# Cosine attention and a highway layer: transposing transfers joined, small work spread over three engines, order rewritten

## The chip, the core and the metric

The kernel runs on one core of one Trainium2 chip. A core has TensorE (PE, matmuls), VectorE (DVE), ScalarE (ACT), GpSimd (POOL) and SyncE (SP, used here to issue DMAs). Each engine works through its own queue in order and waits at semaphores for the others. The metric is the device time of one execution in microseconds; the median of three executions is given.

## The reference

```python
def _attn_ref(q, k, v, tau):                 # q, k, v: (8, 12, 448, 64), float32
    q_n = q / (np.linalg.norm(q, axis=-1, keepdims=True) + 1e-06)
    k_n = k / (np.linalg.norm(k, axis=-1, keepdims=True) + 1e-06)
    scores = np.matmul(q_n, k_n.transpose(0, 1, 3, 2)) / tau
    attn = np.exp(scores - np.max(scores, axis=-1, keepdims=True))
    attn = attn / (np.sum(attn, axis=-1, keepdims=True) + 1e-09)
    return np.matmul(attn, v)

def _moe_ref(x, w_h, w_t, b_t):              # x: (3584, 768), from the attention
    H = np.maximum(x @ w_h, 0.0)
    T = 1.0 / (1.0 + np.exp(-(x @ w_t + b_t)))
    return T * H + (1.0 - T) * x
```

Attention over 8 batches of 12 heads, with q and k brought to length one, and then a gated layer of 768 by 768 on its output.

## The kernel before

**Tiling.** The twelve heads of a batch are worked in six pairs, 48 pairs in all (pair s = 6b + p). The 448 rows of a head are 384 main rows, three to a partition, and a tail of 64. `load_main` brings q and k of a batch in one DMA each from GpSimd's queue (tiles qr, kr, cast to fp16; three buffers each), `load_tails` brings the tails from SP's queue (qt, kt), `load_v` both parts of v (vr, vt).

**Preparation of a batch.** `square` squares q and k for three pairs at a time (tile sq, three buffers; L374 on VectorE, L373 on ScalarE in batch 0), `tail_squares` the tails on ScalarE (L399); `folds` adds the squares up (f at L388 and L390, the last sum at L392); `steps` makes the reciprocal square root, by logarithm and exponential on ScalarE in batch 0, by Newton steps on VectorE after that (rs). `scaled` multiplies q and k of a pair by it on GpSimd (tile qn, L499, four buffers, one pair each), `qtnorm` the tails of q (qtn, L509, GpSimd), `ktnorm` those of k (kb, L518, VectorE). `vcast` and `vtcast` copy v into the tile vp with a column of ones (L626 and L632: VectorE for the main rows of batch 0, ScalarE for the rest).

**Transposes.** In batches 0 to 3 `turn` transposes a pair on TensorE (L540, L543) and copies it out on VectorE (qT, L547). In batches 4 to 7 (`BY_DMA`) it is a transposing DMA on SP's queue: six blocks of 128 by 128 for each pair (L532), and for each batch three blocks of q tails (qtT, L555) and six of k tails (kbT, L558).

**Attention of a pair.** `scores`: three groups of score matmuls (L600) and one for the tail (L614), each followed by its exponential on ScalarE (E at L606, Et at L618). `attend`: the product with v and the row sums (L644, L648, L664), a reciprocal and the division on VectorE (L672, L674) into x, one tile for each batch, in four buffers.

**The layer.** `ffn` takes a batch's x in three groups of 128 rows of 768 and one of the tails. x is transposed (tile xT, three buffers, one group each): by DMA on SP's queue in batches 1 to 6, six or three blocks at a time (L704), by TensorE and VectorE in batches 0 and 7. Matmuls with both weights (L745, tails L729), a tanh on ScalarE for the gate (L768, L769), the relu less x on VectorE (L782), the gate and its product (L787, L790), the sum with x on GpSimd (out, L795; VectorE at the very end), the store from SP's queue (L805, tails in two stores at L801).

**Order.** All of this is first listed as operations (`Plan.op`), each with an engine and what it reads and writes. `ORDER` then gives the order in which all 1723 are issued, and `SLOTS` the buffer that each new tile takes. So the order on every engine and queue is written out by hand, operation by operation. Operations marked `port` on VectorE and GpSimd get one more rule: a GpSimd operation waits for the last marked VectorE operation ahead of it in the order, and where it is in the set `URGENT` the next marked VectorE operation waits for it.

Of the kernel before, what the change touches and what calls it, by code (L numbers as in the profile page):

```python
# [9 lines left out]
FP16 = mybir.dt.float16  # L10
# [92 lines left out]
""".replace("\n", "")  # L103
)

URGENT = frozenset(
    int(n)
    for n in """
116 135 154 155 225 310 336 337 394 413 485 583 621 736 774 811 877 945 963 998 1080 1106 1140 1147 1166 1237
1268 1283 1298 1369 1387 1405 1440 1471 1553 1554 1571 1589 1590 1607 1608 1643 1691  # L110
""".split()
)


class Op:
# [801 lines left out]
```

## Time and profile before

| | |
|---|---|
| median of three executions | 275.48 us (273.61 to 279.13) |
| profiled execution | 274.65 us |
| its span, first to last instruction | 272.8 us |
| granted TensorE clock | 0.994 of full speed |
| chain of waits, by engine | PE 53%, DVE 17%, DMA 14%, ACT 5%, POOL 3%, issue 3%, SP's queue 2% |
| read from and written to memory | 37.82 and 11.01 MB |
| exponentials of the main scores (L606) | 144, 128.5 us of ACT |

The profile comes from one execution. Busy time of an engine is the time in which one of its instructions ran; in a group's row stand the count, the busy time, the mean of one in ns, and behind the second bar the engine's idle time just before them with what ended it. A PE that is busy isn't at its peak, since matmuls overlap: the same kind of matmul shows 323 ns in its row and comes every 82 ns where nothing disturbs it. The chain of waits follows the work that ended last back to what released it, step by step.

### The profile page before, as it was taken

The numbers are of one execution on the slowest core, as the hardware profiler recorded it, in microseconds if no ns is written. First come the engines' busy times: TensorE is split into PE (matmuls) and PEld (weight loads), VectorE is DVE, ScalarE is ACT, GpSimd is POOL, SyncE is SP. The second block draws the span as 40 slices with busy tenths as digits, with TensorE's granted clock in tenths as the row PEclk, the third lists the DMA queues.
The fourth block names the chain that finished last, engine by engine and source line by source line (L and its number), as shares of the span: only waits on it lengthen the run. The fifth ranks groups of instructions, "written<-read, shape, count | busy, mean of one in ns | idle before, by whom it ended". The sixth has DMA issues, their size and how long they took to land.

```text
span 272.8 us, 9106 instructions
## 1 busy us (share of the span) xinstructions
PE 243.6 (89%) x3783; PEld 163.2 (60%) x3783; DVE 198.2 (73%) x446; ACT 209.6 (77%) x312; POOL 159.1 (58%) x172
## 2 busy tenths in 40 slices
PE   0467898999999999999999897998899999999990
PEld 0235475766775676666656574665566767677650
DVE  6577989999989889976876778629853454446464
ACT  2479999879896998789689898797798995683120
POOL 5979656585584775576766564558667464300540
PEclk9999999999999999999999999999999999999997
DMA  7999999999859999996999989999795749620243
GB/s 131 221 192 191 180 207 202 186 194 198 105 78 176 209 164 119 150 171 128 210 157 151 173 191 181 143 190 222 173 167 86 116 124 191 204 90 2 60 178 113
DMA packets 104249, 43.13 MB, mean 158 GB/s; under 512 B 98064, under 2 KB 101136, under 8 KB 104208
## 3 DMA queue, kind: packets, MB, share of 16 engines
q0 software_dynamic: 38464, 16.32, 49.3%
q1 hardware_dynamic: 64512, 25.80, 48.7%
q8 instruction: 30, 0.49, 0.7%
q10 hardware_dynamic: 1232, 0.43, 0.6%
q14 instruction: 11, 0.09, 0.1%
HBM read 37.82 MB, written 11.01 MB: 179 GB/s over the span
## 4 chain that ended last, share of the span: by engine, by line
PE 53%; DVE 17%; DMA 14%; ACT 5%; POOL 3%; issue 3%; SPq 2%; POOLq 0%; ACTq 0%; DVEq 0%
PE pS L745 24%; PE pS L600 7%; PE pB L648 7%; PE pS L729 4%; DMA qT<-qn 4%; DMA qr<-in_q_dram 4%; DMA out_dram<-os 3%; PE pB L664 3%; PE pB L614 3%; PE pB L644 3%; DVE sq L374 2%; POOL qn L499 2%; DMA kr<-in_k_dram 2%; DVE f L388 2%; ACT E L606 2%
## 5 line engine op out<-in xcount | busy, mean ns | idle before, releaser
L606 ACT ACTIVATE E<-pS 128x896 f16<-128x896 f32 x144 | 128.5, 920 | 21.0 <-PE pS L600 18.0
L745 PEld LDWEIGHTS <-xT 64*128 64x128 f16 x1152 | 52.9, 94 | 33.6 <-issue 2.2
L795 POOL TENSOR_TENSOR os<-x,hm 128x768 f32<-128x768 f16 (+1 forms) x30 | 44.2, 1479 | 41.6 <-DVE hm L790 28.5
L745 PE MATMUL pS<-wt,xT 64*128 64x384 f16 x576 | 58.6, 323 | 0.6 <-DMA xT<-x 0.6
L745 PE MATMUL pS<-wh,xT 64*128 64x384 f16 x576 | 57.5, 323 | 0.0
L499 POOL TENSOR_TENSOR qn<-kr,rs 128x384 f16<-128x384 f16 x47 | 39.1, 841 | 30.4 <-DVE rd L672 10.4
L499 POOL TENSOR_TENSOR qn<-qr,rs 128x384 f16<-128x384 f16 x47 | 38.9, 832 | 22.9 <-DVE hm L790 8.3
L600 PE MATMUL pS<-qT 64*128 64x384 f16 x288 | 44.1, 327 | 3.8 <-DMA qT<-qn 1.7
L648 PE MATMUL pB<-vp,E 128*128 128x65 f16 x864 | 43.6, 194 | 0.0
L782 DVE SCALAR_TENSOR_TENSOR hm<-pS,x 128x768 f16<-128x768 f32 (+1 forms) x33 | 27.4, 833 | 19.8 <-PE pS L745 13.6
L648 PEld LDWEIGHTS <-E 128*128 128x128 f16 x864 | 38.5, 98 | 1.2 <-issue 0.7
L600 PEld LDWEIGHTS <-qT 64*128 64x128 f16 x576 | 23.2, 94 | 21.7 <-issue 7.8
L644 PE MATMUL pB<-vp,Et 128*128 128x130 f16 x144 | 32.0, 222 | 0.8 <-ACT Et L618 0.6
L769 ACT ACTIVATE tt<-pS 128x768 f16<-128x768 f32 x24 | 19.5, 813 | 16.3 <-PE pS L745 15.0
L618 ACT ACTIVATE Et<-pB 128x512 f16<-128x512 f32 x48 | 28.5, 603 | 2.9 <-PE pB L614 2.7
L674 DVE SCALAR_TENSOR_TENSOR x<-pB,rd 128x448 f16<-128x448 f32 x48 | 29.7, 620 | 1.1
L600 PE MATMUL pS<-qtT,qT 64*128 64x64 f16 x282 | 27.6, 189 | 0.0
L672 DVE RECIPROCAL rd<-pB 128x7 f32<-128x7 f32 x48 | 9.5, 200 | 22.7 <-PE pB L648 14.4
L280 PE MATMUL pB<-fill 128*128 128x384 f16 x40 | 9.6, 367 | 13.3 <-DVE fill L251 10.7
L626 ACT COPY vp<-vr 128x384 f16<-128x384 f16 x42 | 21.1, 515 | 0.0
L790 DVE TENSOR_TENSOR hm<-tt,hm 128x768 f16<-128x768 f16 (+1 forms) x32 | 18.3, 581 | 2.8 <-POOL os L795 2.6
L664 PE MATMUL pB<-vp,E 128*128 128x65 f16 x288 | 18.3, 194 | 0.2 <-DVE x L674 0.2
(95 smaller groups left out, 382.3 us busy)
## 6 DMA issues: line engine op xcount, KB each, us to landing
out_dram<-os SPq DMA_DIRECT2D x24, 384.0 KB, 3.7
vr<-in_v_dram POOLq DMA_DIRECT2D x8, 576.0 KB, 9.6
kr<-in_k_dram POOLq DMA_DIRECT2D x7, 576.0 KB, 9.8
qr<-in_q_dram POOLq DMA_DIRECT2D x7, 576.0 KB, 11.4
qt<-in_q_dram SPq DMA_DIRECT2D x16, 96.0 KB, 5.8
vt<-in_v_dram SPq DMA_DIRECT2D x16, 96.0 KB, 5.0
out_dram<-os SPq DMA_DIRECT2D x16, 96.0 KB, 2.4
kt<-in_k_dram SPq DMA_DIRECT2D x14, 96.0 KB, 4.9
```

What stands on the lines that cost most here:

```text
L499: return e.tensor_mul(R("qn", s)[:, t].rearrange("l c ab d -> l ab c d"), rows(t, b, p, p + 1)[:, :, 0, :].rearrange("l ab (c d) -> l ab c ...
L600: ins = nc.tensor.matmul(dst, lhsT=qT[ln, 384 + 128 * c : 512 + 128 * c], rhs=rhs, start=True, stop=True)
L606: return nc.scalar.activation(R("E", s)[:, c, :, 0:448], R("S", 3 * s + c)[:, :, 0:448], AF.Exp, scale=inv_tau)
L618: op("ACT", f"expt {s}", lambda: nc.scalar.activation(R("Et", s)[:, 64:576], R("B", ("S", s))[:, :], AF.Exp, scale=inv_tau), key + 3, r=[( ...
L626: return nc.vector.tensor_copy(dst, src) if b == 0 else nc.scalar.copy(dst, src)
L644: nc.tensor.matmul(U[:, 2 * c : 2 * c + 2, :].rearrange("p g e -> p (g e)"), lhsT=Et[:, 128 + 128 * c : 256 + 128 * c], rhs=vp[:, 6:8, :]. ...
L648: ins = nc.tensor.matmul(U[:, 2 * c + ab, :], lhsT=EF[:, j, 576 * ab + 128 * c : 576 * ab + 128 * c + 128], rhs=vp[:, 3 * ab + j, :], star ...
L664: ins = nc.tensor.matmul(U[:, 6, :], lhsT=lt, rhs=rh, start=(n == 0), stop=(n == 7))
L674: op("DVE", f"ev {s}", lambda: nc.vector.scalar_tensor_tensor(out=R("x", b)[:, :, D * p : D * p + D], in0=U_()[:, :, 0:D], scalar=0.0, in1 ...
L745: ins = nc.tensor.matmul(P[:, h, 0:MH], lhsT=lt, rhs=rh, start=(part == 0 and cc == (-1 if wi == 0 else 0)), stop=(part == 1 and cc == CC ...
L782: return nc.vector.scalar_tensor_tensor(out=o_, in0=i0, scalar=0.0, in1=xs, op0=ALU.max, op1=ALU.subtract)
L795: op(en, f"out{wd} {g}", lambda: eng.tensor_add(R("os", g)[:, 0:W], xall(), R("hm", g)[:, 0:W]), at + 0.1, r=[("gg", g), ("x", b)], w=[("o ...
```

## The change

**Transfers joined.** qn now holds two pairs in a tile (two buffers, still four pairs), qT two pairs (three buffers, six pairs for four), and one transposing DMA of twelve blocks turns both. The tails of q stand behind those of k in one tile kb, and one transfer of nine blocks turns them into one tile tT. xT holds two groups in a tile (two buffers), and x of a batch goes in a transfer of twelve blocks and one of nine. The tail rows of the result are stored in one DMA for two.

**Engines.** A set `MOVED` names 146 operations that go to another engine than their usual one; `pick(one, other)` looks it up as an operation is listed. The usual engine of v's copies and of the tail squares in batches 0 or 1 changes too. In numbers, before and after:

| operations | before | after |
|---|---|---|
| products of q and k (L499) | POOL 94, DVE 2 | POOL 45, DVE 51 |
| tails of q; of k (halves) | POOL 8; DVE 16 | POOL 2, DVE 6; DVE 7, POOL 9 |
| squares of three pairs, half each | DVE 28, ACT 2 | DVE 15, ACT 15 |
| squares of tails | ACT 16 | ACT 12, DVE 4 |
| sums of squares (L388, L390) | DVE 46 | DVE 34, POOL 12 |
| copies of v (main); (tails) | ACT 42, DVE 6; ACT 16 | ACT 20, DVE 24, POOL 4; ACT 8, DVE 6, POOL 2 |
| copies of a transposed pair (L547) | DVE 24 | DVE 18, ACT 6 |
| sums with x (full; tails) | POOL 23, DVE 1; POOL 7, DVE 1 | POOL 10, DVE 14; POOL 5, DVE 3 |
| clears of E, Et, kb | DVE 8 | DVE 1, POOL 7 |

**Buffers and order.** x goes from four buffers to three. The product with v waits for the clears of all three E and Et buffers, for one of each before. `ORDER`, `SLOTS` and `URGENT` (43 operations before, 57 after) are new throughout; there are 1687 operations for 1723.

```diff
-    NR = dict(qr=3, kr=3, qt=2, kt=2, kb=2, vr=3, vt=2, vp=2, sq=3, f1=2, f2=2, n2=2, rs=3, qn=4,
-              qtn=2, qtT=2, qT=4, kbT=2, E=3, Et=3, rd=2, x=4, xT=3, tt=3, hm=3, os=4, S=3, B=2)
+    NR = dict(qr=3, kr=3, qt=2, kt=2, kb=2, vr=3, vt=2, vp=2, sq=3, f1=2, f2=2, n2=2, rs=3, qn=2,
+              qT=3, tT=2, E=3, Et=3, rd=2, x=3, xT=2, tt=3, hm=3, os=4, S=3, B=2)
...
+    def pick(one, other):
+        return other if len(pl.ops) in MOVED else one
+    def product(eng, out_, a, c):
+        return (nc.vector if eng == "DVE" else nc.gpsimd).tensor_mul(out_, a, c)
+    def copied(eng, out_, a):
+        return nc.scalar.copy(out_, a) if eng == "ACT" else (nc.vector if eng == "DVE" else nc.gpsimd).tensor_copy(out_, a)
...
+            eng = pick(eng, "DVE" if eng == "ACT" else "POOL" if b == 1 else "ACT")
...
     def scaled(t, b, p, key, eng):
         s = 6 * b + p
-        e = nc.vector if eng == "DVE" else nc.gpsimd
+        eng = pick(eng, "DVE")
...
         if b in BY_DMA:
-            op("SP", f"xd6 q {s}", lambda: nc.sync.dma_start(
-                R("qT", s)[:, 0:768].rearrange("p (c l) -> p c l", c=6), R("qn", s).rearrange("l t c ab d -> l (t c ab d)"),
-                transpose=True), key, r=[("qn", s)], w=[("qT", s)])
+            if p % 2 == 0:
+                m = s // 2
+                op("SP", f"xd12 q {m}", lambda: nc.sync.dma_start(
+                    R("qT", m)[:, 1:13, :], R("qn", m).rearrange("l x t c ab d -> l (x t c ab d)"),
+                    transpose=True), key, r=[("qn", m, 0), ("qn", m, 1)], w=[("qT", m, 0), ("qT", m, 1)])
             return
...
-            op("SP", f"xd3 t {b}", lambda: nc.sync.dma_start(
-                R("qtT", b)[:, :, :], R("qtn", b).rearrange("l j ab d -> l (j ab d)"), transpose=True), key,
-               r=[("qtn", b)], w=[("qtT", b)])
-            op("SP", f"xd6 k {b}", lambda: nc.sync.dma_start(
-                R("kbT", b)[:, :, :], R("kb", b).rearrange("l p ab d -> l (p ab d)"), transpose=True), key,
-               r=[("kb", b)], w=[("kbT", b)])
+            op("SP", f"xd9 t {b}", lambda: nc.sync.dma_start(
+                R("tT", b)[:, :, :], R("kb", b).rearrange("l p ab d -> l (p ab d)"), transpose=True), key,
+               r=[("kb", b, 0), ("kb", b, 1)], w=[("tT", b)])
...
+        eng = pick(*(("DVE", "POOL") if b < 2 else ("ACT", "DVE")))
...
-            op("SP", f"xd{nb} {g}", lambda: nc.sync.dma_start(R("xT", g)[:, 0:nb, :], xall(), transpose=True), key,
-               r=[("x", b)], w=[("xT", g)])
+            if not i % 2:
+                hf = i // 2
+                nd = 12 - 3 * hf
+                op("SP", f"xd{nd} {b} {hf}", lambda: nc.sync.dma_start(
+                    R("xT", (b, hf))[:, 0:nd, :], R("x", b)[:, 4 * hf : 4 + 3 * hf, :].rearrange("l h m -> l (h m)"),
+                    transpose=True), key, r=[("x", b)], w=[("xT", (b, hf), 0), ("xT", (b, hf), 1)])
...
-            for h in range(2):
-                op("SP", f"sth {g} {h}", lambda h=h: nc.sync.dma_start(
-                    rows_[384:448, MH * h : MH * h + MH], R("os", g)[64 * h : 64 * h + 64, 0:MH]), at + 0.4,
-                   r=[("os", g)], w=[("o", g)])
+            op("SP", f"sth {g}", lambda: nc.sync.dma_start(
+                rows_[384:448].rearrange("l (h m) -> h l m", h=2), R("os", g)[:, 0:MH]), at + 0.4,
+               r=[("os", g)], w=[("o", g)])
```

More of the change, by code (lines that the diff above doesn't have):

```diff
@@ L108 @@
     for n in """
-116 135 154 155 225 310 336 337 394 413 485 583 621 736 774 811 877 945 963 998 1080 1106 1140 1147 1166 1237
-1268 1283 1298 1369 1387 1405 1440 1471 1553 1554 1571 1589 1590 1607 1608 1643 1691
+225 241 316 336 355 374 443 482 523 542 561 599 618 649 678 688 729 748 766 767 805 823 824 869 884 894 934 1003
+1004 1051 1065 1080 1090 1148 1164 1183 1199 1200 1218 1247 1261 1276 1319 1326 1344 1360 1361 1482 1515 1521
+1539 1540 1557 1574 1575 1591 1592
+""".split()
+)
+MOVED = frozenset(
+    int(n)
+    for n in """
[6 rows of a table added]
 """.split()
@@ L213 @@
         rs=ring("rs", NR["rs"], [128, 3, NN], FP32),
-        qn=ring("qn", NR["qn"], [128, 2, NCH, 2, D], FP16),
-        kbT=ring("kbT", NR["kbT"], [128, NP, 128], FP16),
-        qtn=ring("qtn", NR["qtn"], [128, 3, 2, D], FP16),
-        qtT=ring("qtT", NR["qtT"], [128, 3, 128], FP16),
-        qT=ring("qT", NR["qT"], [128, 896], FP16),
+        qn=ring("qn", NR["qn"], [128, 2, 2, NCH, 2, D], FP16),
+        tT=ring("tT", NR["tT"], [128, NP + 3, 128], FP16),
+        qT=ring("qT", NR["qT"], [128, 14, 128], FP16),
         E=ring("E", NR["E"], [128, NCH, 2, 512], FP16),
@@ L237, with squared @@
     op = pl.op
+    def pick(one, other):
[4 more added lines that the diff above has]
+        return nc.scalar.copy(out_, a) if eng == "ACT" else (nc.vector if eng == "DVE" else nc.gpsimd).tensor_copy(out_, a)
+    def squared(eng, out_, a):
+        return nc.scalar.activation(out_, a, AF.Square) if eng == "ACT" else product(eng, out_, a, a)
     def R(name, i):
@@ L248, in clear, with fn @@
         for n, t in enumerate(tiles):
-            def fn(t=t):
+            eng = pick("DVE", "POOL") if name in ("zE", "zEt", "zvp", "zkb") else "DVE"
+            e = nc.vector if eng == "DVE" else nc.gpsimd
+            def fn(t=t, e=e):
                 for vw, x in views(t):
-                    ins = nc.vector.memset(vw, x)
+                    ins = e.memset(vw, x)
                 return ins
-            op("DVE", f"{name} {n}", fn, key + gap * n, w=[(name, n)])
+            op(eng, f"{name} {n}", fn, key + gap * n, w=[(name, n)])
     op("POOL", "ident", lambda: make_identity(nc, ident), 5, w=[("id", 0)])
@@ L371, in fn @@
                 d = R("sq", i)[:, g0:g1, :].rearrange("l (p a c) d -> l a p (c d)", a=4, c=NCH)[:, 2 * t : 2 * t + 2]
-                if eng == "ACT":
-                    return nc.scalar.activation(d, a, AF.Square)
-                return nc.vector.tensor_mul(d, a, a)
+                return squared(eng, d, a)
             op(eng, f"sq{p1 - p0} {b} {p0} {t}", fn, key,
-               r=[rowtok(t, b, p) for p in range(p0, p1)] + ([("tab", 0)] if eng == "ACT" else []), w=[("sq", i)], port=eng == "DVE")
+               r=[rowtok(t, b, p) for p in range(p0, p1)] + [("tab", 0)], w=[("sq", i)], port=eng != "ACT")
         if tails:
@@ L387, in folds @@
         w0, w1 = ("fa",) + i, ("fb",) + i
-        op("DVE", f"fa{n} {b} {i[1]}", lambda: nc.vector.tensor_add(v_("f1"), v_("sq")[:, :, 0:32], v_("sq")[:, :, 32:64]),
+        eng = pick("DVE", "POOL")
+        e1 = nc.vector if eng == "DVE" else nc.gpsimd
+        op(eng, f"fa{n} {b} {i[1]}", lambda: e1.tensor_add(v_("f1"), v_("sq")[:, :, 0:32], v_("sq")[:, :, 32:64]),
            key, r=[("sq", i)], w=[w0], u=[("f1", i)], port=True)
-        op("DVE", f"fb{n} {b} {i[1]}", lambda: nc.vector.tensor_add(v_("f2"), v_("f1")[:, :, 0:16], v_("f1")[:, :, 16:32]),
+        eng = pick("DVE", "POOL")
+        e2 = nc.vector if eng == "DVE" else nc.gpsimd
+        op(eng, f"fb{n} {b} {i[1]}", lambda: e2.tensor_add(v_("f2"), v_("f1")[:, :, 0:16], v_("f1")[:, :, 16:32]),
            key, r=[w0], w=[w1], u=[("f1", i), ("f2", i)], port=True)
@@ L395, in tail_squares, with fn @@
     def tail_squares(b, i, key):
-        def fn(t):
+        def fn(t, eng):
             sq = R("sq", i)[:, 6 * t : 6 * t + 6].rearrange("l g d -> l (g d)")
             a = R("qt", b).rearrange("l ab p d -> l (ab p d)") if t == 0 else R("kt", b).rearrange("l p d -> l (p d)")
-            return nc.scalar.activation(sq, a, AF.Square)
+            return squared(eng, sq, a)
         for t in range(2):
-            op("ACT", f"sqt {b} {t}", lambda t=t: fn(t), key, r=[("qt", b) if t == 0 else ("kt", b)] + ([("tab", 0)] if b == 0 else []),
-               w=[("sq", i)])
+            eng = pick(*(("DVE", "POOL") if b == 1 else ("ACT", "DVE")))
+            op(eng, f"sqt {b} {t}", lambda t=t, eng=eng: fn(t, eng), key,
+               r=[("qt", b) if t == 0 else ("kt", b)] + ([("tab", 0)] if b == 0 else []), w=[("sq", i)], port=eng != "ACT")
     def square_tail(b, key):
@@ L495, in scaled @@
         s = 6 * b + p
-        e = nc.vector if eng == "DVE" else nc.gpsimd
+        eng = pick(eng, "DVE")
         def fn():
-            return e.tensor_mul(
-                R("qn", s)[:, t].rearrange("l c ab d -> l ab c d"),
+            return product(
+                eng, R("qn", s // 2)[:, s % 2, t].rearrange("l c ab d -> l ab c d"),
                 rows(t, b, p, p + 1)[:, :, 0, :].rearrange("l ab (c d) -> l ab c d", c=NCH),
@@ L505, in scaled, with fn @@
         op(eng, f"{'qk'[t]}n {s}", fn, key, r=[rowtok(t, b, p), ("rn", b, p)], u=[("rs", b)],
-           w=[("qn", s)], port=True)
+           w=[("qn", s // 2, s % 2)], port=True)
     def qtnorm(b, key):
-        op("POOL", f"qtn {b}", lambda: nc.gpsimd.tensor_mul(
-            R("qtn", b).rearrange("l j ab d -> l ab j d"), R("qt", b)[:, :, :, :],
+        eng = pick("POOL", "DVE")
+        op(eng, f"qtn {b}", lambda: product(
+            eng, R("kb", b)[:, NP : NP + 3].rearrange("l j ab d -> l ab j d"), R("qt", b)[:, :, :, :],
             rtails(b).unsqueeze(3).to_broadcast([128, 2, 3, D])), key, r=[("qt", b), ("rn", b, 6)],
-           u=[("rs", b)], w=[("qtn", b)], port=True)
+           u=[("rs", b)], w=[("kb", b, 1)], port=True)
     def ktnorm(b, key):
         for ab in range(2):
-            def fn(ab=ab):
+            eng = pick("DVE", "POOL")
+            def fn(ab=ab, eng=eng):
                 ln = slice(64 * ab, 64 * ab + 64)
-                return nc.vector.tensor_mul(R("kb", b)[ln, :, ab, :], R("kt", b)[ln, :, :],
+                return product(eng, R("kb", b)[ln, 0:NP, ab, :], R("kt", b)[ln, :, :],
                                             R("rs", b)[ln, 0, 6:12].unsqueeze(2).to_broadcast([64, NP, D]))
-            op("DVE", f"kb {b} {ab}", fn, key, r=[("kt", b), ("zkb", min(b, 1)), ("rn", b, 6)], u=[("rs", b)],
-               w=[("kb", b)], port=True)
+            op(eng, f"kb {b} {ab}", fn, key, r=[("kt", b), ("zkb", min(b, 1)), ("rn", b, 6)], u=[("rs", b)],
+               w=[("kb", b, 0)], port=True)
     tn = [0]
@@ L610, in ft @@
         def ft():
-            qT, S_ = R("qT", s), R("B", ("S", s))
-            keys = R("kbT", b)[:, p] if b in BY_DMA else qT[:, 768:896]
-            for dst, rhs in ((S_[:, 0:64], tails()), (S_[:, 64:448], qT[:, 0:384]), (S_[:, 448:512], tails())):
+            S_ = R("B", ("S", s))
+            qT = R("qT", s // 2)[:, 1 + 6 * z : 4 + 6 * z].rearrange("p c l -> p (c l)")
+            keys = R("tT", b)[:, p] if b in BY_DMA else R("qT", s // 2)[:, 13 * z]
+            for dst, rhs in ((S_[:, 0:64], tails()), (S_[:, 64:448], qT), (S_[:, 448:512], tails())):
                 ins = nc.tensor.matmul(dst, lhsT=keys, rhs=rhs, start=True, stop=True)
             return ins
-        op("PE", f"qkt {s}", ft, key + 3, mode="F", r=tok + ([("kbT", b)] if b in BY_DMA else []), w=[("B", ("S", s))])
+        op("PE", f"qkt {s}", ft, key + 3, mode="F", r=tok, w=[("B", ("S", s))])
         op("ACT", f"expt {s}", lambda: nc.scalar.activation(
@@ L625, in fn @@
             dst = R("vp", b)[:, p, 0:6, 0:D].rearrange("l (ab c) d -> l ab c d", ab=2)
-            return nc.vector.tensor_copy(dst, src) if b == 0 else nc.scalar.copy(dst, src)
-        op("DVE" if b == 0 else "ACT", f"vc {b} {p}", fn, key, r=[("vr", b), ("zvp", min(b, 1))], w=[("vp", b, p)], port=b == 0)
+            return copied(eng, dst, src)
+        op(eng, f"vc {b} {p}", fn, key, r=[("vr", b), ("zvp", min(b, 1))], w=[("vp", b, p)], port=eng != "ACT")
     def vtcast(b, key):
         for ab in range(2):
-            op("ACT", f"vtc {b} {ab}", lambda ab=ab: nc.scalar.copy(
-                R("vp", b)[64 * ab : 64 * ab + 64, :, 6 + ab, 0:D], R("vt", b)[64 * ab : 64 * ab + 64, :, :]),
-               key, r=[("vt", b), ("zvp", min(b, 1))], w=[("vp", b, 6)])
+            eng = pick(*(("DVE", "POOL") if b < 2 else ("ACT", "DVE")))
+            op(eng, f"vtc {b} {ab}", lambda ab=ab, eng=eng: copied(
+                eng, R("vp", b)[64 * ab : 64 * ab + 64, :, 6 + ab, 0:D], R("vt", b)[64 * ab : 64 * ab + 64, :, :]),
+               key, r=[("vt", b), ("zvp", min(b, 1))], w=[("vp", b, 6)], port=eng != "ACT")
     def attend(b, p, key):
@@ L666, in tail @@
             return ins
-        rd = [("E", s), ("Et", s), ("vp", b, p), ("vp", b, 6), ("zE", min(s, 2)), ("zEt", min(s, 2))]
+        rd = [("E", s), ("Et", s), ("vp", b, p), ("vp", b, 6)] + [(z, n) for z in ("zE", "zEt") for n in range(3)]
         for c in range(NCH):
@@ L793, in ffn @@
         last = b == B - 1 and i >= 2
-        eng, en = (nc.vector, "DVE") if last else (nc.gpsimd, "POOL")
+        en = "DVE" if last else pick("POOL", "DVE")
+        eng = nc.vector if en == "DVE" else nc.gpsimd
         op(en, f"out{wd} {g}", lambda: eng.tensor_add(R("os", g)[:, 0:W], xall(), R("hm", g)[:, 0:W]), at + 0.1,
```

71 lines of the change are left out of this document (38 added, 33 removed), and 140 rows, old and new, of tables (MOVED, ORDER).

## The prediction

> **What bounds the kernel now.** I read the page first, for the engines' totals, then the table of windows for where TensorE stands still, then the chain of waits inside those windows, then the groups for prices.
>
> ```profile
> PE 243.6 (89%) x3783; PEld 163.2 (60%) x3783; DVE 198.2 (73%) x446; ACT 209.6 (77%) x312; POOL 159.1 (58%) x172
> ```
> ```profile
> 0.00:20.00 20.00, 7.32 (x50) 3.83 (x50) 13.68 (x48) 9.58 (x18) 15.49 (x25) 1.00 1.24 181
> 20.00:40.00 20.00, 16.47 (x259) 11.17 (x260) 17.62 (x44) 18.35 (x28) 13.56 (x17) 1.00 1.44 192
> 40.00:60.00 20.00, 19.00 (x325) 13.53 (x323) 18.85 (x47) 17.20 (x25) 13.15 (x16) 1.00 1.37 194
> ...
> 100.00:120.00 20.00, 19.62 (x314) 13.06 (x314) 19.03 (x40) 16.82 (x27) 11.57 (x12) 1.00 1.16 141
> 120.00:140.00 20.00, 19.25 (x302) 12.40 (x300) 14.67 (x35) 17.12 (x27) 14.61 (x16) 1.00 0.85 167
> 140.00:160.00 20.00, 19.31 (x309) 12.74 (x306) 12.58 (x26) 17.44 (x25) 12.43 (x13) 1.00 1.40 189
> 160.00:180.00 20.00, 18.49 (x314) 12.62 (x313) 14.26 (x32) 16.59 (x26) 10.69 (x12) 1.00 1.08 150
> 180.00:200.00 20.00, 17.80 (x285) 12.03 (x283) 15.66 (x31) 16.88 (x28) 12.36 (x13) 1.00 1.06 196
> 200.00:220.00 20.00, 20.00 (x325) 13.54 (x322) 9.04 (x21) 18.69 (x27) 14.11 (x15) 1.00 0.77 121
> ```
>
> The columns are the stretch, its length, then busy time of PE, weight load, DVE, ACT, POOL, the granted clock, DMA. TensorE is the fullest engine, at full clock. Three stages differ. In the first 40 us it idles 12.68 + 3.53 us. From 40 to 120 it is nearly always busy, but DVE is too (18.85 and 19.03 of 20), so there VectorE sets the pace. From 120 to 200 DVE is light (12.6 to 15.7 of 20), and yet TensorE idles 0.75 + 0.69 + 1.51 + 2.20 = 5.15 us: those are waits, not load. From 200 on the loss is gone. The chain of waits says what they are (start, us, what):
>
> ```profile
> 138.45 10.09 DMA qr<-in_q_dram
> 148.56 0.51 DVE sq L374
> ...
> 151.56 2.41 POOL qn L499 x3
> 153.98 0.80 SPq L532
> 154.87 0.63 SPq L337
> 155.55 2.74 DMA out_dram<-os
> 158.29 4.36 DMA qT<-qn
> 162.82 1.64 POOL qn L499 x3
> 164.46 5.93 DMA qT<-qn
> ```
>
> This is the stage in which q and k are turned by DMA: SP's queue, a store, a transfer, GpSimd making the next products, a transfer again. At its head DVE stands before a square whose load is still under way.
>
> **The transfers.** Landing (the last number, us), and two issues on SP's queue:
>
> ```profile
> qT<-qn SPq DMA_TRANSPOSE x24, 3.6
> ```
> ```profile
> 115.67 1.20 SPq L555 DMA_TRANSPOSE qtT<-qtn  x1
> ...
> 120.76 1.27 SPq L532 DMA_TRANSPOSE qT<-qn  x1
> ```
>
> A transfer of 3 blocks holds SP 1.20 us, one of 6 blocks 1.27, so I take 1.4 for 12 (0.023 a block). There are 24 + 24 + 4 + 4 = 56 such issues, about 70 us of SP; afterwards 12 + 12 + 4 = 28, about 38. Eight tail stores go too. SP is in order, so the stores and small loads behind a transfer come sooner, and GpSimd's wait for a store buffer shortens. Landing of 12 blocks is not in the trace: not under the 3.6 of 6 blocks, and at most double, 7.2. I take 4.6, near the lower end, because doubling blocks from 3 to 6 hardly moved the issue. The Trainium skill (DMA: Bandwidth & Descriptors, Anatomy of one DMA) has a fixed 2.0 us and bytes over 436 GB/s; by that an estimate for 12 blocks (393 KB) is 2.9 us against 2.45 for 6, which would make the step 0.45 us instead of my 1.0 and change the sum by less than a microsecond.
>
> The price of joining is that a pair of heads waits for the later of its four products. The order written into the kernel leaves room for it. Matmul work runs at
>
> ```profile
> 251.69 12.29 PE pS L745 x150
> ```
>
> 82 ns each when nothing disturbs it. Counted so, the TensorE work between the issue of a q/k transfer and the first score that reads it is at least 4.4 us before (head pair 33) and 5.1 us after (pair 38: 50 matmuls of 82 ns, four score groups of two such matmuls and two short ones, about 0.19 each, one more of 0.2). The squares of the last batch also move: between the issue of the loads of batch 7 and the first square on DVE that reads them lie about 10 us of such work before and 16 after, so the 2.2 us that DVE idles ahead of the square at 148.56 should go. What is late next is the products themselves, on DVE and POOL. Of the 5.15 us I count three quarters back, **-4**; all of it, -5.2, and none, 0, are the ends. The idle DVE before the late square is part of that and not counted again.
>
> **The work moved between engines.** Prices, by form (count, then busy us and mean ns of one):
>
> ```profile
> L499 POOL TENSOR_TENSOR qn<-kr,rs 128x384 f16<-128x384 f16 x47 | 39.1, 841 | 30.4 <-DVE rd L672 10.4 <-DVE kb L518 7.7 <-DVE f L390 2.4
> ...
> L795 POOL TENSOR_TENSOR os<-x,hm 128x768 f32<-128x768 f16 x23 | 38.0, 1653 | 41.1 <-DVE hm L790 28.1 <-DMA out_dram<-os 7.6 <-DVE f L390 3.0
> ```
> ```profile
> L547 DVE COPY qT<-pB 128x896 f16<-128x896 f16 x24 | 14.5, 612 | 4.9 <-PE pB L543 2.5 <-ACT E L606 2.3
> ...
> L374 DVE TENSOR_TENSOR sq<-kr 128x1152 f16<-128x1152 f16 x14 | 12.0, 859 | 0.1
> ...
> L518 DVE TENSOR_TENSOR kb<-kt,rs 64x384 f16<-64x384 f32 x16 | 9.8, 613 | 0.4
> ...
> L626 DVE COPY vp<-vr 128x384 f16<-128x384 f16 x6 | 2.0, 325 | 0.0
> ...
> L470 DVE TENSOR_TENSOR qn<-first,first_rs 128x384 f16<-128x384 f32 x2 | 1.1, 550 | 0.0
> L795 DVE TENSOR_TENSOR os<-x,hm 128x768 f32<-128x768 f16 x1 | 1.0, 957 | 0.0
> ```
> ```profile
> L626 ACT COPY vp<-vr 128x384 f16<-128x384 f16 x42 | 21.1, 515 | 0.0
> ...
> L373 ACT ACTIVATE sq<-kr 128x1152 f16<-128x1152 f16 x1 | 1.1, 1147 | 0.0
> ```
>
> Off POOL to DVE: 49 products at 0.84 (41.2 us; the nearest DVE row, with a wider input, is 0.55: 27.0), 13 full sums at 1.65 (21.5; 0.96: 12.4), 2 half sums and 6 q-tail products at about 0.9 (7; 0.55: 4.4). POOL -69.7, DVE +43.8. To DVE from ACT: 18 copies of v at 0.33 and 12 smaller things (6 tails of v, 4 tail squares, a square, at 0.33 to 0.61), +11. Off DVE to ACT: 13 squares at 0.82 to 0.86 and 6 copies at 0.61, -14.5. Off DVE to POOL: 9 k-tail products at 0.61 and 12 of the sums of squares (0.3 to 0.84 each), -11. Those and 6 copies cost POOL, at its 0.84 for 384 elements and in proportion up to 1152 and down to 192, +23 (a one-input copy may cost less than a product; ends 15 and 25). Sums: DVE 198 + 29 = 227, POOL 159 - 47 = 112, ACT -22 x 0.52 - 8 x 0.52 - 4 x 0.52 - 0.8 + 13 x 1.15 + 6 x 0.92 = +2.
>
> Whether that helps depends on how the two engines share their path to memory. One row decides for me:
>
> ```profile
> 158.64 1.64 POOL L795 TENSOR_TENSOR os<-x,hm 128x768 f32<-128x768 f16 x1 [0.61 <-DMA out_dram<-os]
> ```
> ```profile
> 159.26 1.62 DVE L374 TENSOR_TENSOR sq<-kr 128x1152 f16<-128x1152 f16 x1
> ```
>
> The square lasts 1.62 us where its fellows average 0.86, and ends 0.6 after the GpSimd sum does: it stood still for it. So for products, sums and squares the two engines' time adds up, and the kernel's code besides makes each GpSimd operation wait for the VectorE one ahead of it. Together they fall by 47 - 29 = 18 us, half of it past 120 us, where load is not the limit. By the place of the moved operations in the new order, up to the point that the kernel before reaches at 120 us DVE gains 24 products and 4 q tails (28 x 0.55), 3 full sums (3 x 0.96), 11 copies and tails of v and 5 squares (16 x 0.3 to 0.6): about 25; it loses 11 squares (9.0), 6 copies (3.7), 5 k tails (3.1), 7 sums of squares and some clears (3.5): about 19. POOL loses 28 x 0.84 + 3 x 1.65 = 28.5 and gains about 15. So there DVE alone gets 6 us fuller, and both together 7 us emptier. The row above speaks for the sum, and part of what DVE is busy with today is standing still; but the copies, evacuations and reductions of DVE count for DVE alone. I take **-2** (ends -5 and +6).
>
> A rule speaks against this part. Loads of q, k and v are issued by GpSimd, and their row now is
>
> ```profile
> qr<-in_q_dram POOLq DMA_DIRECT2D x7, 576.0 KB, 11.4
> ```
>
> with DVE at 95% for long stretches. The Trainium skill (SBUF — State Buffer, SBUF: two separate sides) says that while VectorE runs an instruction that uses two ports GpSimd "cannot write the descriptors", so that a load stalls. By that rule 24 more copies on VectorE would delay loads; no run here shows it yet.
>
> **Start and end.** In the start the first pair's squares go ahead of the next pair's on ACT, worth up to 1; seven clears go to GpSimd between its first loads, at a few tenths each, and cost up to 1.5; six copies leave a full DVE for an ACT that is just as full. Net 0, ends -1.5 and +1.5. At the end one store of the last half rows goes instead of two:
>
> ```profile
> 268.97 1.11 SPq L801 DMA_DIRECT2D out_dram<-os  x2
> ```
>
> half of 1.11 saved, **-0.5**. The x buffers (three for four) hold a batch until its last sum; the next use of a buffer lies about 4 us of TensorE work behind that sum at the tightest (batches 3 and 6). I cost it at nothing; if that cover goes, it is one wait of a few microseconds for each.
>
> **Sum.** -4 - 2 + 0 - 0.5 = -6.5 on the profiled span of 272.8, and the profiled execution took 274.65, so 268.1. The median of the runs shown, 275.48, is 0.8 above the profiled execution, so **268.5**, 2.5% less. A change can be told from none at about 2% here, 5.5 us: 270.0 and 281.0 are the marks.
>
> **Rivals.** *Hidden anyway, 274.* TensorE is busy 89% and what waits is passed on: the transfer stage loses its queueing and gains the wait for the second head, and VectorE, now at 227, is as full until 200 us as it is until 120. For it: the pace from 40 to 120 with a full DVE is little better than from 120 to 200. Against: the 5.15 us idle there come with DVE at 63 to 78%. It leaves -1 to -2.
>
> *The joined transfer lands late, 283.* If 12 blocks take 7.2 us under load rather than 4.6, the six or seven transfers whose scores follow within 5.1 to 7.3 us of TensorE work make it stand 1 to 2 us each: 7 x 1.5 = 10.5, less the 3 saved elsewhere. It decides from a landing of about 6 us. For it: two transfers on the chain already took 4.36 and 5.93. Against: the bytes are the same and the queue is shorter.
>
> *Loads come late, 285.* Mechanism and place: GpSimd's loads, issued between more VectorE copies, land well after the 11.4 us of now; DVE stands at a square as at 148.56 and holds everything behind it. At 2.2 us a time for five batches that is +11, less 1 to 2. It decides once a load takes more than the 16 us of work now planned behind it. Against: the copies last 0.33 each and the loads are issued earlier than their squares by more than before. By the Trainium skill's rule above (SBUF — State Buffer) this is where the copies would lead.
>
> *The change does more than I count, 262:* if the stage from 40 to 200 us ran as the one from 200 on, without idling, TensorE would win 1.0 + 0.4 + 5.2 and the start 1.5 besides, and VectorE's stage its full 5.
>
> **How the numbers follow.** My forecast and the stronger gain together 0.56 (the latter 0.13), hidden anyway 0.22, late joined transfers 0.13, late loads 0.09. Predicted is the likeliest, 268.5. The range 260 to 284 leaves out the far half of the stronger gain and most of the late loads. Faster by more than 2% has 0.55, slower by more than 2% 0.21, the rest 0.24. The likeliest case's own range is 264 to 272.
>
> **What would show it.** Right: PE idle between 120 and 200 us under 2 us, no DMA of q among the chain's long pieces, SP's transfers 28 with a landing under 5 us, DVE near 227 busy, POOL near 112. Wrong: waits of TensorE for qT that add up to several microseconds, a landing over 6 us, idle time of DVE before a square put down to a load, or more idle time of TensorE in the first 40 us than now.

## The result, and the profile after

| | before | after |
|---|---|---|
| median of four executions | 275.62 us (273.61 to 279.13) | 289.43 us (286.48 to 291.37) |
| ratio, 95% interval | | 1.0446 [1.0324, 1.0568], slower |
| profiled execution, its span | 274.65, 272.8 us | 291.37, 289.6 us |

Here and below, medians are of all executions, while ratios and intervals leave out those over 1.5% above the fastest of the same kernel, of which the profiled execution of the kernel after is one.

The engines' totals of the kernel after:

```profile
PE 250.1 (86%) x3783; PEld 167.8 (58%) x3783; DVE 218.0 (75%) x494; ACT 211.7 (73%) x296; POOL 117.4 (41%) x140
```

The work moved about as counted (DVE 218 for 227 forecast, POOL 117 for 112, ACT +2), and yet the kernel lost 14 us. The table of windows (columns as before) shows where:

```profile
100.00:120.00 20.00, 20.00 (x342) 14.12 (x340) 17.90 (x42) 19.11 (x29) 8.89 (x10) 1.00 1.07 179
120.00:140.00 20.00, 18.21 (x294) 12.51 (x291) 16.08 (x33) 17.17 (x27) 12.47 (x12) 1.00 1.20 167
140.00:160.00 20.00, 18.83 (x298) 12.74 (x295) 14.34 (x31) 17.82 (x27) 6.10 (x7) 1.00 1.57 137
160.00:180.00 20.00, 14.12 (x229) 9.55 (x228) 13.78 (x33) 11.46 (x18) 6.84 (x7) 0.83 0.81 150
180.00:200.00 20.00, 15.88 (x202) 10.19 (x200) 12.91 (x29) 11.10 (x16) 4.11 (x4) 0.83 1.03 148
```

Up to 120 us TensorE is about as busy as before. From 120 to 200 it idles 1.79 + 1.17 + 5.88 + 4.12 = 12.96 us where it idled 5.15, and its granted clock falls to a mean of 0.83 for 40 us. The long pieces of the chain of waits name transfers:

```profile
126.55 7.19 DMA qT<-qn
...
153.20 5.84 SPq L594
...
159.21 7.39 DMA qT<-qn
...
177.43 13.02 DMA vr<-in_v_dram
...
238.54 7.57 DMA xT<-x
```

This looks like two of the rivals at once: twelve blocks that land after 7.2 to 7.6 us, and a late load of v. But the transfer at 126.55 has no load of GpSimd's queue beside it. What runs there instead is seen in the same table cut into single microseconds, in its last two columns (mean busy share of the 16 DMA engines, GB/s):

```profile
122.50:123.50 1.00, 0.66 (x12) 0.40 (x10) 1.00 (x2) 1.00 (x2) 0.75 (x1) 1.00 1.14 424
...
124.00:125.00 1.00, 1.00 (x23) 0.67 (x19) 0.98 (x2) 0.79 (x1) 0.78 (x1) 1.00 4.72 75
125.00:126.00 1.00, 1.00 (x29) 0.93 (x25) 1.00 (x3) 1.00 (x3) 0.00 (x0) 1.00 0.13 49
126.00:127.00 1.00, 1.00 (x20) 0.62 (x18) 0.97 (x4) 0.82 (x2) 0.32 (x1) 1.00 0.13 49
...
160.00:161.00 1.00, 0.53 (x16) 0.41 (x13) 0.00 (x0) 1.00 (x2) 0.00 (x0) 1.00 0.13 49
...
286.00:287.00 1.00, 0.00 (x0) 0.00 (x0) 0.00 (x0) 0.00 (x0) 0.00 (x0) 0.50 0.13 49
```

While a transfer of q waits (126 and 160 us), and again at the very end, the share is 0.13: 2 of 16 is 0.125. A packet counts in the stretch in which it begins, with all of its time. So the 4.72 from 124 to 125 us is made of packets that began there and stayed open long after, and from 125 us on next to nothing begins but the packets of one DMA. SP's queue tells which DMA that is. In front of the slow transfers, and as the last one of the kernel, stands the store of the tail rows, now one for two (L849):

```profile
120.52 0.67 SPq L849 DMA_DIRECT2D out_dram<-os  x1
121.30 3.61 SPq L594 DMA_TRANSPOSE tT<-kb  x1
125.00 0.65 SPq L352 DMA_DIRECT2D qt<-in_q_dram  x1
125.78 0.59 SPq L356 DMA_DIRECT2D kt<-in_k_dram  x1
126.55 3.84 SPq L567 DMA_TRANSPOSE qT<-qn  x1
```

In the trace its 128 packets of 1,536 bytes begin over 3.9 to 5.0 us in each of the eight batches, two at a time; the 64 of each of the two stores before began over 0.25 to 1.2 us. What this does to a transposing transfer is clearest where no load of tails runs beside it. A tail store's packets run from 240.04 to 244.01 us, beside the transfer of x issued at 238.54. From 242.75 to 243.75 us none of the transfer's packets begins, and some 20 that began before stay open; the others begin from 244 us on. Plain transfers go on beside such a store: from 178 to 180 us some 100 packets of the stores of main rows begin. In the list of DMA issues no landing time stands behind the new store, as one did behind the two before (2.4 us):

```profile
out_dram<-os SPq DMA_DIRECT2D x24, 384.0 KB, 4.2
...
out_dram<-os SPq DMA_DIRECT2D x8, 192.0 KB
```

### The profile page after: what moved, and what is told of

It reads as the page before. It is cut to its first block, busy times and chain, and to the rows that moved or that the text cites. A ratio compares the mean times of both kernels' runs of the same rounds, so it can differ in the third digit from the quotient of the medians.

```text
span 289.6 us, 9053 instructions
## 1 busy us (share of the span) xinstructions
PE 250.1 (86%) x3783; PEld 167.8 (58%) x3783; DVE 218.0 (75%) x494; ACT 211.7 (73%) x296; POOL 117.4 (41%) x140
## 4 chain that ended last, share of the span: by engine, by line
PE 53%; DVE 16%; DMA 14%; ACT 5%; issue 4%; POOL 3%; SPq 2%; DVEq 0%; ACTq 0%; POOLq 0%
PE pS L793 23%; PE pS L637 7%; PE pB L689 6%; DMA qT<-qn 5%; PE pS L777 5%; DMA vr<-in_v_dram 4%; PE pB L652 3%; PE pB L705 3%; PE pB L577 3%; DMA xT<-x 3%; PE pB L685 2%; ACT E L643 2%; SPq L594 2%; DVE qn L253 2%; DMA kr<-in_k_dram 2%
## 5 line engine op out<-in xcount | busy, mean ns | idle before, releaser
L793 PEld LDWEIGHTS <-xT 64*128 64x128 f16 x1152 | 55.1, 96 | 34.5 <-issue 2.3
L793 PE MATMUL pS<-wh,xT 64*128 64x384 f16 x576 | 59.3, 335 | 0.5 <-DVE hm L830 0.5
L793 PE MATMUL pS<-wt,xT 64*128 64x384 f16 x576 | 56.8, 323 | 0.7 <-DMA xT<-x 0.7
L689 PE MATMUL pB<-vp,E 128*128 128x65 f16 x864 | 45.0, 196 | 0.0
L844 POOL TENSOR_TENSOR os<-x,hm 128x768 f32<-128x768 f16 (+1 forms) x15 | 21.0, 1397 | 45.8 <-DVE hm L838 26.7
L253 POOL TENSOR_TENSOR qn<-qr,rs 128x384 f16<-128x384 f16 x25 | 21.0, 840 | 38.9 <-DVE rd L713 10.0
L637 PE MATMUL pS<-tT,qT 64*128 64x64 f16 x282 | 28.0, 192 | 0.0
L253 POOL TENSOR_TENSOR qn<-kr,rs 128x384 f16<-128x384 f16 x20 | 16.8, 846 | 21.4 <-DVE qn L253 17.1
L844 DVE TENSOR_TENSOR os<-x,hm 128x768 f32<-128x768 f16 (+1 forms) x17 | 15.2, 892 | 9.1 <-DMA out_dram<-os 9.0
L705 PE MATMUL pB<-vp,E 128*128 128x65 f16 x288 | 18.4, 195 | 0.3 <-DVE x L715 0.3
L685 PEld LDWEIGHTS <-Et 128*128 128x128 f16 x144 | 14.2, 98 | 6.0 <-issue 3.9
## 6 DMA issues: line engine op xcount, KB each, us to landing
vr<-in_v_dram POOLq DMA_DIRECT2D x8, 576.0 KB, 15.1
```

Source lines behind the costliest of these rows:

```text
L253: return (nc.vector if eng == "DVE" else nc.gpsimd).tensor_mul(out_, a, c)
L637: ins = nc.tensor.matmul(dst, lhsT=qT[ln, 384 + 128 * c : 512 + 128 * c], rhs=rhs, start=True, stop=True)
L685: nc.tensor.matmul(U[:, 2 * c : 2 * c + 2, :].rearrange("p g e -> p (g e)"), lhsT=Et[:, 128 + 128 * c : 256 + 128 * c], rhs=vp[:, 6:8, :]. ...
L689: ins = nc.tensor.matmul(U[:, 2 * c + ab, :], lhsT=EF[:, j, 576 * ab + 128 * c : 576 * ab + 128 * c + 128], rhs=vp[:, 3 * ab + j, :], star ...
L705: ins = nc.tensor.matmul(U[:, 6, :], lhsT=lt, rhs=rh, start=(n == 0), stop=(n == 7))
L793: ins = nc.tensor.matmul(P[:, h, 0:MH], lhsT=lt, rhs=rh, start=(part == 0 and cc == (-1 if wi == 0 else 0)), stop=(part == 1 and cc == CC ...
```

## The experiments

Three theories stood after this. A: the joined tail store runs on two DMA engines and holds up what needs all sixteen. B: twelve blocks land late by themselves. C: loads come late and hold VectorE.

**Store and transfers, one at a time.** On the changed kernel, two tail stores again:

```diff
-            op("SP", f"sth {g}", lambda: nc.sync.dma_start(
-                rows_[384:448].rearrange("l (h m) -> h l m", h=2), R("os", g)[:, 0:MH]), at + 0.4,
-               r=[("os", g)], w=[("o", g)])
+            def sth():
+                for h in range(2):
+                    ins = nc.sync.dma_start(rows_[384:448, MH * h : MH * h + MH], R("os", g)[64 * h : 64 * h + 64, 0:MH])
+                return ins
+            op("SP", f"sth {g}", sth, at + 0.4, r=[("os", g)], w=[("o", g)])
```

> The changed kernel with the tail rows of each result stored in two DMAs again, all else as changed. Theory A, the joined tail store: in the trace of the changed kernel each one's 128 packets run for 3.9 to 5.0 us (0.25 to 1.2 us for the separate ones before), the transposing transfers behind them land late, and the last one ends the kernel 4.8 us after its issue. Then the time falls by the 3.5 us at the end and by most of the 14 us lost by the end of batch 5: 270 to 277 us. Theory B, twelve blocks land late by themselves and a pair waits for four products: only the end is won, 284 to 287. Theory C, loads of v and k that come late and hold VectorE in its queue: as B, 284 to 287.

On the kernel before, the joined store alone:

```diff
+                    if g not in stored:
+                        stored.add(g)
+                        return nc.sync.dma_start(rows_[384:448].rearrange("l (h m) -> h l m", h=2), R("os", g)[:, 0:MH])
```

> The kernel before with the tail rows stored in one DMA for two, as in the changed kernel, and nothing else changed. Theory A: the stores alone cost 3.5 us at the end and several of the seven others hold a transfer of 6 blocks for up to 4 us: 281 to 290 us. Theories B and C: only the end, 278 to 280.

On the changed kernel, each joined transfer issued as two from its old place (for q and k; the others alike), with the joined tail stores and without:

```diff
+                    for z in range(2):
+                        ins = nc.sync.dma_start(R("qT", m)[:, 1 + 6 * z : 7 + 6 * z, :],
+                                                R("qn", m)[:, z].rearrange("l t c ab d -> l (t c ab d)"), transpose=True)
```

> The changed kernel with every joined transposing transfer issued as two again (6 and 6, 6 and 3 blocks), the joined tail stores kept. Theory A: little is won, 285 to 291. Theory B: the first pair gets its half sooner and the time goes to 272 to 278. Theory C: as it is, 287 to 291.

> Both edits of the two runs before on the changed kernel: two tail stores and all transfers split. What is left of the change is the new order, the engines and the buffers. Theory A: within 3 us of the run with two tail stores alone. Theory B: well below that run, by over 6 us. Theory C: both runs stay above 283.

| run | median us | ratio to before, interval |
|---|---|---|
| two tail stores | 273.26 (270.85 to 274.70) | 0.9851 [0.9755, 0.9948] |
| kernel before, joined store | 286.90 (285.18 to 287.84) | 1.0332 [1.0237, 1.0426] |
| all transfers split, joined store | 290.53 (289.49 to 294.47) | 1.0471 [1.0383, 1.0558] |
| all transfers split, two tail stores | 278.25 (275.38 to 281.83) | 1.0039 [0.9989, 1.0089] |

The kernel before took 276.47 beside them. The store alone costs some 10 us on the kernel before and 14 to 16 on the changed one (ratio 1.0446 against 0.9851, or against 0.9914 and 0.9922 in two runs further down whose tail rows ran in the same way). Splitting the transfers repairs nothing, though the two halves still wait for the products of both pairs. B falls as the cause, and C with it, since the store alone brings the time back. With two tail stores the changed kernel comes out some 1 to 1.5% below the kernel before.

**The end and the middle.** The joined store in the last batch alone, on the kernel with two:

```diff
+                if b == B - 1:
+                    return nc.sync.dma_start(rows_[384:448].rearrange("l (h m) -> h l m", h=2), R("os", g)[:, 0:MH])
```

> The changed kernel with two tail stores in batches 0 to 6 and the joined one in batch 7 alone. If the joined store costs its own length at the end and the rest in the middle, this is 3 to 4 us above the run with two tail stores everywhere (273.3), so 276 to 277.5; the other 12 us come from the seven stores in the middle. If the last store alone were the trouble, 285 or more.

Median 278.25 us (273.94 to 280.19), ratio 0.9876 [0.9816, 0.9936]. The seven executions spread too widely for 3 us, so the trace decides. The tail rows begin to go out at the same moment, 270.0 and 269.9 us, and end at 274.9 with the joined store and at 271.2 with two; the spans are 276.2 and 272.9. After 270 us only the store runs. First the run with the joined one, then that without, from their tables of windows:

```profile
270.00:271.00 1.00, 0.00 (x0) 0.00 (x0) 0.00 (x0) 0.00 (x0) 0.00 (x0) 0.98 0.15 37
...
274.00:275.00 1.00, 0.00 (x0) 0.00 (x0) 0.00 (x0) 0.00 (x0) 0.00 (x0) 0.50 0.11 41
```
```profile
270.00:271.00 1.00, 0.00 (x0) 0.00 (x0) 0.00 (x0) 0.00 (x0) 0.00 (x0) 0.79 0.79 178
271.00:272.00 1.00, 0.00 (x0) 0.00 (x0) 0.00 (x0) 0.00 (x0) 0.00 (x0) 0.50 0.04 9
```

So 3.3 us of the loss are the end; by subtraction the other 11 to 13 lie in the seven stores before.

**Queue or engines?** The joined store from ScalarE's queue. In a first form, for batches 0 to 6, it was also put 36 operations later:

> The changed kernel with the joined tail stores of batches 0 to 6 issued from ScalarE's queue, 36 operations later in the order so that ScalarE does not wait for their data; the last one stays on SP's queue. If the transposing transfers stand behind the stores because they are in the same queue, the cost in the middle goes and only the end's 3.5 us and some ScalarE issue time are left: 276 to 280. If any transfer that needs the engines on which the store runs is held up, whatever the queue: 283 to 290.

It took 296.62 us, but nothing follows: in batches 1, 4 and 5 that place is behind the next sum into the same buffer, so other rows were stored, and ScalarE waited for that sum. In its old place, for batches 0 to 4:

```diff
+            e, en = (nc.scalar, "ACT") if b < 5 else (nc.sync, "SP")
-            op("SP", f"sth {g}", lambda: nc.sync.dma_start(
+            op(en, f"sth {g}", lambda: e.dma_start(
```

> The changed kernel with the joined tail stores of batches 0 to 4 issued from ScalarE's queue at their old place in the order, each well after its data and before the next use of its buffer; batches 5 to 7, behind which few transfers follow, stay on SP's queue. If the transposing transfers are held up because they stand behind the stores in the same queue: 276 to 282. If a store that runs on few engines holds up the transfers of any queue: 285 to 291.

292.78 us, 1.0628 [1.0571, 1.0684]: no better for another queue. In its chain a transfer of q takes

```profile
156.23 9.09 DMA qT<-qn
```

with the store's packets running from 156.0 to 161.5 in the other queue. From 159 to 161.5 us some 100 to 125 packets of SP's queue begin in each half microsecond; in the next three it is 400 to 570. It is the engines that are shared.

**Number of engines, or one larger DMA?** Two stores, each with its 64 rows as blocks (2 of 32, 4 of 16):

```diff
-                    ins = nc.sync.dma_start(rows_[384:448, MH * h : MH * h + MH], R("os", g)[64 * h : 64 * h + 64, 0:MH])
+                    ins = nc.sync.dma_start(rows_[384:448, MH * h : MH * h + MH].rearrange("(a l) m -> a l m", a=2), R("os", g)[64 * h : 64 * h + 64, 0:MH])
```

> The changed kernel with two tail stores, each written with its 64 rows as 2 blocks of 32, so that the pattern's outermost dimension is 2 as in the joined store (h); the bytes and the number of stores are those of the run at 273.3. If the outermost dimension of 2 puts a store on two DMA engines and that alone is the cause, its 64 packets run for about 2 us on two engines, two such stores for 4 us, and the time is that of the changed kernel: 284 to 291. If joining (one DMA of 192 KB, its one landing) is the cause: 272 to 276.

> The same with 4 blocks of 16 rows. If the outermost dimension sets the number of engines, each store runs on four for about 1 us, and a good half of the 16 us of loss goes: 275 to 281. If joining is the cause: 272 to 276.

275.06 and 275.18 us, 0.9914 [0.9867, 0.9962] and 0.9922 [0.9878, 0.9965], but this decided nothing: the packets of a pair of stores ran 0.6 to 2.4 us, spread as ever, as if blocks of adjacent rows were one run of rows again. With every second or fourth row instead (`"(l a) m -> a l m"`), which puts the tail rows of the result in another order:

> The changed kernel with two tail stores, each written as 2 groups of 32 rows, even rows and odd rows, which are not next to each other, so that the outermost dimension of 2 stays (in the two runs before, blocks of consecutive rows ran spread as ever, 0.7 to 2.4 us for the 128 packets). The tail rows of the result come in another order by this. If an outermost dimension of 2 puts a store on two DMA engines and that alone is the cause: the 128 packets of a pair of stores take 4 us or more and the time is 284 to 291. If joining (one DMA of 192 KB with one landing) is the cause: 272 to 276.

> The same with 4 groups of 16 rows, every fourth row; the tail rows come in another order. If the outermost dimension sets the number of engines, each pair of stores takes about 2 us on four engines and a good half of the loss goes: 275 to 281. If joining is the cause: 272 to 276.

| tail rows of a batch | DMA engines | the 128 packets begin over, us | median us | ratio to before, interval |
|---|---|---|---|---|
| two stores | 16 | 0.6 to 2.1 | 273.26 | 0.9851 [0.9755, 0.9948] |
| two stores, every fourth row | 4 | 1.9 to 3.2 | 279.60 | 1.0117 [0.9982, 1.0252] |
| joined store | 2 | 3.9 to 5.0 | 289.43 | 1.0446 [1.0324, 1.0568] |
| two stores, even and odd rows | 2 | 4.4 to 5.6 | 296.20 | 1.0721 [1.0532, 1.0911] |

The last kind took 292.80 to 356.11 us in four executions, and its ratio rests on two of them. The share of the DMA engines in the last store shows the count, 2 of 16 (0.125) and 4 of 16 (0.25), in the windows of the run with even and odd rows and of that with every fourth row:

```profile
285.00:286.00 1.00, 0.00 (x0) 0.00 (x0) 0.00 (x0) 0.00 (x0) 0.00 (x0) 0.50 0.13 35
```
```profile
275.00:276.00 1.00, 0.00 (x0) 0.00 (x0) 0.00 (x0) 0.00 (x0) 0.00 (x0) 0.50 0.27 100
```

Two stores bring the loss back, and more, when they run on two engines, and a third to a half of it on four. Joining as such is not the cause. A joined store that runs on all sixteen was not tried.

**What the rest of the change is worth.** On the changed kernel with two tail stores, some of the transfers split:

> The changed kernel with two tail stores, and the joined transfers of q and k and of the tails issued as two again; those of x stay joined. With all of them split it took 278.3, with none split 273.3. If the gain of joining lies in q and k (the transfers that the scores wait for): 276 to 279. If it lies in SP's queue as a whole: half of it, 275 to 276. If in x: 272 to 275.

> The changed kernel with two tail stores, and the joined transfers of x issued as two again; those of q, k and the tails stay joined. If the gain of joining lies in q and k: 272 to 275. If in SP's queue as a whole: 275 to 276. If in x: 276 to 279.

278.71 us, 1.0043 [0.9989, 1.0096], and 274.09, 0.9909 [0.9861, 0.9957]. The gain of joining lies in q, k and the tails; joining x shows no gain that could be told (0.9909 and 0.9851 have intervals that overlap). Then the moves, undone by taking numbers out of `MOVED`:

> The changed kernel with two tail stores, and of the 146 moved operations the 42 between VectorE and ScalarE back on their usual engine (20 copies of v, 3 small squares to ScalarE; 13 squares and 6 copies of a transposed pair to VectorE). VectorE gets some 5 us more, ScalarE about as much as before. If VectorE's load sets the pace until 120 us: 275 to 278. If these moves make no difference: 272 to 275. If the copies of v on VectorE delay GpSimd's loads: 268 to 272.

> The changed kernel with two tail stores, and of the 146 moved operations the 104 between GpSimd and VectorE back on their usual engine (72 products and sums to GpSimd, 32 smaller ones mostly to VectorE). By the prediction's step these moves gain by freeing the two engines together of 18 us: 275 to 278 without them. If they gain nothing, as the comparison of the run with transfers split and two tail stores (278.3) and the kernel before (276.5) leaves open: 271 to 274.

284.86 us (281.92 to 286.74) and 290.25 (285.79 to 291.95): by the two shortest executions of each some 10 and 15 us more than the run with two tail stores, far past what any of the theories gave. The order was written for the moved operations, so this prices the moves under that order, not the moves. Their worth together with the order and the buffers is the run with all transfers split and two tail stores: 1.0039 [0.9989, 1.0089], nothing that can be told. Last, the start:

```diff
+        more = {11: 2, 12: 1, 4: 2, 5: 1, 16: 2, 15: 1, 13: 2, 3: 1, 18: 2, 10: 1, 17: 2}.get(i, 0)
-            for _ in range(n):
+            for _ in range(n + more):
```

> The changed kernel with two tail stores, and 39 warming matmuls for the 22 that TensorE runs from 2.8 to 9.0 us, so that it isn't idle for 5.4 us before its first work at 14.4 us. In the run with two tail stores the granted clock is 0.5 from 12 to 18 us, behind that idle time, and in the kernel before it is 1.0. If the clock there is on the path: 1 to 2 us less, 271 to 272.5. If the first 40 us are set by VectorE, ScalarE and the loads: 273 to 274, as without.

275.30 us (271.76 to 276.41), 0.9918 [0.9876, 0.9959]. It doesn't test what it was made for: the longer warm-up ends at 11.3 us, before the first work, and the clock falls all the same (0.50 from 14 to 20 us in its table of windows).

## Why the prediction was wrong, point by point

**The step that failed: the end store, "-0.5".** It took "half of 1.11 saved", an issue time, for the whole of the edit, and counted the eight stores that go ("Eight tail stores go too") as relief for SP's queue; no row was sought for how the joined store would run. Measured, joining the tail stores costs 14 to 16 us: 3.3 at the end, 11 to 13 in between, as transposing transfers behind or beside it wait for two engines and TensorE for them. The Trainium skill (DMA: Bandwidth & Descriptors, Why a DMA increments its semaphore by 16 and not by 1) has the rule: a DMA runs on the largest number of engines up to 16 that divides the slowest dimension of both its patterns. Here `h l m` puts the 2 outermost. The trace agrees: 0.13 of the engines with an outermost 2, 0.27 with a 4. The prediction drew on that page for the landing of a transfer and not for the one pattern that the change had turned round.

**Transfers joined, "-4".** The size was near: 1.0039 with all of them split, 0.9851 to 0.9922 joined, so 3 to 5 us. The time for which a transfer of twelve blocks holds SP was too: forecast 1.4 us, in the run with two tail stores 1.36 at least and 1.5 in the median. So was the landing, once nothing held it up; in the same run:

```profile
qT<-qn SPq DMA_TRANSPOSE x12, 4.0
```

against 4.6 taken. The formula of the Trainium skill (DMA: Bandwidth & Descriptors, Anatomy of one DMA) gave 2.9, too little; the page fits it for DMAs that GpSimd issues, and these are SP's. Its step of 0.45 from six blocks to twelve is nearer to the measured 0.4 (3.6 to 4.0) than the 1.0 taken. Where the gain would come from was confirmed in part at most: TensorE's idle time from 120 to 200 us should have gone down, and in that run it is 0.27 + 3.11 + 0.46 + 1.88 = 5.72 us, against 5.15 before:

```profile
120.00:140.00 20.00, 19.73 (x318) 13.85 (x312) 18.66 (x39) 18.74 (x29) 11.16 (x11) 1.00 1.03 186
140.00:160.00 20.00, 16.89 (x280) 11.56 (x277) 14.78 (x32) 16.57 (x24) 5.83 (x6) 1.00 1.43 151
160.00:180.00 20.00, 19.54 (x312) 13.36 (x313) 17.01 (x41) 16.81 (x24) 8.48 (x9) 0.91 0.96 157
180.00:200.00 20.00, 18.12 (x299) 12.47 (x295) 15.63 (x35) 14.51 (x22) 7.38 (x7) 1.00 0.72 163
```

With the same order and all transfers split it is 7.28 us. So joining alone took 1.6 us off this stage in these two executions, whose spans are 272.9 and 274.1, and what else changed had put more on. The joined one took 274.68 us, the second longest of its four, and shows no gain over the kernel before at all; where the shorter ones win is open.

**Work moved, "-2".** With order and buffers it came to +0.4% [-0.1%, +0.9%], some 1 us, inside the ends -5 to +6. The busy times were near, the benefit wasn't there: that term was mis-sized too. **The start and x in three buffers, 0 each,** were not tried alone, and the longer warm-up says nothing of the start.

**The sum.** Two slips in it change nothing: 275.48 less 6.5 is 269.0, not 268.5, and the smaller things that go from ScalarE to VectorE, as listed, are 11 and not 12.

**The rivals.** "Hidden anyway" comes nearest to the kernel with the store repaired: TensorE's idle time in the transfer stage stayed, and 1 to 1.5% is less than the 2.5% forecast. "The joined transfer lands late, 283" fits the symptom, landings above 6 us and waits of TensorE, but not the cause: twelve blocks land after 4.0 us, and splitting them did not help. "Loads come late" is partly real and outlives the repair; the chain of the run with two tail stores still holds

```profile
151.75 8.68 DMA qT<-qn
...
170.89 10.79 DMA vr<-in_v_dram
```

and its loads of v land after 12.4 us (9.6 before, 15.1 after). Whether that comes from copies on VectorE was not settled: with 20 of them back on ScalarE the loads of v land after 11.1 us, but other operations moved with them. The range, 260 to 284, ended short because none of the cases had the tail store as a cost.

## What to carry to other kernels

Price a joined DMA by how it runs, not by the issue it saves: look at the outermost dimension of both patterns, and if that is 2, expect it on two engines unless the rows adjoin. A DMA on few engines is paid for by others that need all of them, here the transposing transfers above all, whichever queue it comes from. The chain of waits then names the victims; it was a low share of the DMA engines at the moment of the wait that pointed to the culprit. Operations that were moved and an order made for them are one edit; undoing one alone prices neither.

## What the runs showed of the hardware

**The clock after a wait.** In the kernel after TensorE stands still from about 160.5 to 166.6 us, but for one small matmul at 165.4:

```profile
162.50:165.00 2.50, 0.00 (x0) 0.00 (x0) 2.44 (x6) 0.00 (x0) 0.00 (x0) 0.80 1.33 90
165.00:167.50 2.50, 1.08 (x9) 0.46 (x11) 2.42 (x6) 0.23 (x1) 0.18 (x1) 0.50 1.19 247
167.50:170.00 2.50, 2.50 (x22) 1.15 (x19) 1.46 (x4) 1.17 (x2) 2.22 (x3) 0.50 0.91 244
170.00:172.50 2.50, 2.50 (x51) 2.07 (x51) 1.40 (x3) 2.16 (x3) 1.17 (x2) 0.84 0.13 49
```

Its granted clock falls to half some 3.5 us into the wait (0.80 is 1.5 us of 2.5 at full speed) and stays there until about 171, so the first 4 us of work are worth 2 (twelve matmuls of L793 take 2.11 us at 167.5 and took 1.14 at 157.9). By this estimate a wait of 6 us costs 8. The Trainium skill (TensorE: Matmul & The Clock Gate, HAM oscillation — how this bites in real kernels) warns of gaps over about 3.4 us, and this row agrees. **Adjacent rows.** A pattern given as 2 or 4 blocks of adjacent rows ran spread over the engines as the plain one did; only rows that don't adjoin kept the outer dimension.
